# RWKV-7 attention followed by a cosine-gated MLP: the running product of the decays taken on four chunks at once, by a product tree and over DRAM

## The chip, the cores and the metric

The kernel runs on one core of a Trainium2 chip. The metric is device time in microseconds, the median of several executions of the program. TensorE is called PE, VectorE DVE, ScalarE ACT, GpSimd POOL, and SyncE, which here only issues DMAs, SP. PEld is PE's loading of weights, which overlaps its matmuls.

## What is computed

```python
# r, k, v, w, a, b: (4, 8, 768, 40) float32; w between 0.85 and 0.95
for t in range(S):
    y[:, :, t] = einsum('bhd,bhde->bhe', r_t, state)
    Sa = einsum('bhde,bhe->bhd', state, a_t)
    state = state * w_t[:, :, None, :] - einsum('bhd,bhe->bhde', Sa, b_t) + einsum('bhd,bhe->bhde', v_t, k_t)
x = y.transpose(0, 2, 1, 3).reshape(3072, 320)
h = x @ w_in                 # 320 x 2048
out = (h * cos(h)) @ w_out   # 2048 x 320
```

`moe_w_in` and `moe_w_out` come as 64-bit floats and are rounded to 32 bits on the chip.

## The kernel before

The 768 steps are cut into 24 chunks of 32. A chunk's natural layout (`nat`) has 128 partitions, 4 batches times 32 steps, and 8 heads times 64 places (40 used) along the row; the transposed layout has two heads' places on the partitions and 128 columns (batch, step) for each of four head pairs.

Within a chunk the recurrence becomes matrix algebra, for which the running product W of the decays w over the steps of the chunk is needed in both layouts: in the transposed one to scale a (`aT`), the result (`yt`) and the state (`wc`, the last column), and in the natural one as its reciprocal `rw`, which scales b (`bn`) and k (`kn`).

The work before the recurrence goes by pairs of chunks and is called p1. Its steps are:

- `p1_w(c)`: PE transposes w of both chunks into one PSUM tile `wT` (line 298). ACT copies the first column of each chunk aside (line 336), DVE clears it in PSUM (line 337), and a DVE scan multiplies along the steps (line 340) into `wb`. POOL copies the last columns to `wc`.
- `p1_a(c)`, once for each chunk: PE transposes the scanned `wb` back (`wn`, line 353) and a (`aps`, line 298), both into halves of one PSUM tile; DVE takes the reciprocal of `wn` (line 361) and multiplies `aps` by the product shifted by one step (line 363); POOL multiplies b by the reciprocal (line 366).
- `p1_b(c)` and `p1_n(c)`: `bn` is transposed, copied by ACT, and multiplied with `aT` (`nps`); ACT copies the result to `nt`.

For each four chunks DVE inverts the triangular matrices that come of `nt`: a transpose (`u`, line 406), 31 steps of a product and a subtraction each (lines 414 and 418), and a transpose to `rt` (line 422). `p2` prepares v, r, k of a chunk (`vT`, `rT`, `kT`, `gram`), and `main(c)` is the recurrence proper in five steps: `ch_t` transposes the state (`sT`), then `ch_q`, `ch_x` (`x0ps`), `ch_s` (`sps`, which needs `rt`) and `ch_z` (`dps`, which gives the new state `qz` and the output `yt`). The output goes through DRAM (`xd`) to the layout of the MLP (`xT`).

The MLP is cut into pieces: `first_a` and `first_b` (`ph`), turned into `gT` on ACT and DVE (`turns`), and `second` (`po`). While the recurrence goes on, a piece is put at each place marked M in the list of a chunk's segments, which is written out by hand (`segs`). All engines run their instructions in the order in which this list issues them. `later(n, work)` issues work n steps on. Until chunk 3 the pieces wait for the rounding of the weights (`words`, `mant`, `expo`, lines 205 to 232).

Eight PSUM banks are used: `at()` gives out two tiles of two banks in turn, and `ps_h` and `ps_o` two of one bank each, which hold `ph` and `po`, and in the start-up `wn` and `aps` too. A tile is given out again only when all have read it.

SP issues nearly all loads; the first loads of a go out from ACT and POOL. `shifted(n)` puts n one-column matmuls on PE, before chunk 2 (56) and chunk 19 (48). `busy` puts idle matmuls on PE in the start-up.

The order of the start-up, before chunk 0, is

```python
first, other = p1(0), p1(2)
for seg in (*first[:3], *other[:3], *first[3:], *other[3:]):
    step(seg)
```

Of the kernel before, what the change touches and what calls it, by code (L numbers as in the profile page):

```python
# [20 lines left out]
def kernel(  # L21
# [68 lines left out]
    def kept(name, shape, n=1, fill=None, part=lambda t: t, on=nc.gpsimd):  # L90

        tiles = []
        for i in range(n):
            t = const.tile(shape, F32, tag=f"{name}{i}", name=f"{name}{i}")
            if fill is not None:
                on.memset(part(t), fill)
            tiles.append(t)
        return tiles
# [47 lines left out]
    def load(c, names, via=nc.sync):  # L146
        for n in names:
            for i in range(B):
                via.dma_start(
                    nat[n, c][blk[i], :, :D],  # L150
                    src[n][i, :, c * C : (c + 1) * C, :].rearrange("h t d -> t h d"),
                )

    for c in range(2):
        load(c, "w")
        load(c, "a", nc.scalar)
    for n, c in (("b", 0), ("b", 1), ("w", 2), ("w", 3), ("b", 2), ("b", 3)):
        load(c, n)
    load(0, "kvr")


# [2 lines left out]
    for i in range(4):  # L164
# [1 line left out]
            su[blk[i]], su[blk[i]], pattern=[[0, HH], [1, C]], compare_op=ALU.is_gt, fill=0.0,  # L166
            base=0, channel_multiplier=-1,
        )
    load(2, "a", nc.gpsimd)
    load(3, "a", nc.gpsimd)  # L170
    half_pi = kept("half_pi", [P, 1], 1, math.pi / 2)[0]
    warm = kept("warm", [P, 1])[0]
    nc.scalar.activation(warm, half_pi, ACTF.Sin)
    rnd = kept("rnd", [P, 1], 1, ROUND)[0]
    w1 = kept("w1", [P, 4 * B, C], 2, 0.0, on=nc.vector)
    bn_b = kept("bn", [P, H, DP], 7, 0.0, padding, nc.vector)
    kn_b = kept("kn", [P, H, DP], 2, 0.0, padding, nc.vector)

    by_in = kept("by_in", [P, 1], 1, 0.5 / math.pi)[0]
    by_out = kept("by_out", [P, 1], 1, 2.0 * math.pi)[0]  # L180
# [1 line left out]


    BF16 = mybir.dt.bfloat16
    idle = const.tile([P, 512], BF16, tag="idle", name="idle")
    nc.gpsimd.memset(idle, 0.0)
    tick = const.tile([P, 1], BF16, tag="tick", name="tick")

# [103 lines left out]
    def at(name):  # L292
        return ps_a.tile([P, 2, 512], F32, tag="at", name=name)

    def turned(ps, x):

        for i in range(4):
            nc.tensor.transpose(  # L298
                ps[:, i * P : (i + 1) * P], x[:, 2 * i : 2 * i + 2].rearrange("p e d -> p (e d)"), ident
            )  # L300
# [10 lines left out]
    def later(steps, work):  # L311
        waiting.append([steps, work])
# [17 lines left out]
    def p1_w(c):  # L330
        ps = at("wT")
        for i in range(2):
            turned(ps[:, i], nat["w", c + i])

        for i in range(2):
            nc.scalar.copy(w1[i][:, :, 0:1], b4(ps[:, i])[:, :, 0:1])
        nc.vector.memset(ps[:, :, ::C], 0.0)
        for i in range(2):
            wb = ring.tile([P, 4 * P + 1], F32, tag="wb", name="wb")
            nc.vector.tensor_tensor_scan(wb[:, 1:], ps[:, i], flat(w1[i]), 0.0, ALU.mult, ALU.add)  # L340
            wc = ring.tile([P, 4 * B], F32, tag="wc", name="wc")
            nc.gpsimd.tensor_copy(wc, wb[:, C::C])
            G["wb", c + i], G["wc", c + i] = wb, wc

    def p1_a(c):
        if c < 4:
            wn = ps_h.tile([P, 512], F32, tag="h", name="wn")
            aps = ps_o.tile([P, 512], F32, tag="o", name="aps")
        else:
            ps = at("wn")  # L350
            wn, aps = ps[:, 0], ps[:, 1]
        for j in range(4):
            nc.tensor.transpose(
                wn[:, j * P : (j + 1) * P], G["wb", c][:, j * P + 1 : (j + 1) * P + 1], ident
            )

        nc.gpsimd.memset(G["wb", c][:, : 4 * P : C], 1.0)
        G["wx", c] = b4(G["wb", c][:, : 4 * P])
        turned(aps, nat["a", c])
        rw = ring.tile([P, H, D], F32, tag="rw", name="rw")  # L360
        nc.vector.reciprocal(rw, unpad(wn.rearrange("p (h d) -> p h d", h=H)))  # L361
        aT = ring.tile([P, 4, P], F32, tag="aT", name="aT")
        nc.vector.tensor_tensor(
            aT.rearrange("p j (b t) -> p (j b) t", b=B), b4(aps), G["wx", c], ALU.mult
        )
        nc.gpsimd.tensor_tensor(unpad(bn_b[c % 7]), unpad(nat["b", c]), rw, ALU.mult)
        G["rw", c], G["aT", c] = rw, aT

    def p1_b(c):
        ps = at("bT")  # L370
# [204 lines left out]
    def ch_z(c):  # L575
# [3 lines left out]
        for bb in range(B):  # L579
            for e in range(2):  # L580
                mm(
                    ps[bb // 2][full[e], bb % 2, : 4 * N72], idle[blk[bb], :DP],
                    idle[blk[bb], : 4 * N72], True,
                )
        for s, n in ((0, kn_b[c % 2]), (1, bn_b[c % 7])):
            for j in range(4):
# [145 lines left out]
    def p1(c):  # L732


        def first_w():
            p1_w(c)
            if c == 4:
                for i in range(2):
                    later(1, lambda i=i: load(6 + i, "w"))

        def an_a(i):
            p1_a(c + i)
            if c == 4:
                later(1, lambda: load(6 + i, "ab"))
            elif i and c >= 2 and c + 3 < NCH:
                for m in range(6):
                    later(
                        9 + m // 3 if c == 2 else 2 + m, lambda m=m: load(c + 2 + m % 2, "wab"[m // 2])
                    )

        return [first_w, lambda: an_a(0), lambda: an_a(1), lambda: p1_b(c), lambda: p1_n(c)]

    def p2(c):
        def last():
# [14 lines left out]
    with tc.manual_schedule():  # L769
# [24 lines left out]
        def busy(n, after=False):  # L794


            ps = ps_h.tile([P, 512], F32, tag="h", name="busy")
            if after:
                nc.vector.memset(tick, 1.0)
                nc.tensor.matmul(  # L800
                    ps[:1, :], lhsT=tick, rhs=idle, start=True, stop=True, skip_group_check=True
                )
            for _ in range(n):
                mm(ps, idle[:, :P], idle, True)

        def shifted(n):

# [4 lines left out]


        first, other = p1(0), p1(2)
        for seg in (*first[:3], *other[:3], *first[3:], *other[3:]):
            step(seg)
        p2_in(0)
        p2_kn(0)
        inv_steps.extend(inverse(0))
# [2 lines left out]
        for n, seg in ((12, v), (0, k), (0, g), (6, main(0)[2]), (6, None), (4, v1), (0, k1), (0, g1)):  # L822
            for _ in range(n):
                inv_steps.pop(0)()
            if seg:
                step(seg)
            else:
                for m in range(3):
                    w_work[m][0]()
                p2_in(1)  # L830
                p2_kn(1)
        while inv_steps:
            inv_steps.pop(0)()
            if 2 < len(inv_steps) < 9:
                busy(1, True)
# [13 lines left out]
        def allowed(c):  # L849
            return done < len(pieces) and 2 * pieces[done][0] + 2 <= c  # L850

        N_PAD = {2: 56, 19: 48}
        M = object()
        for c in range(NCH):
            t, q, x, s, z = main(c)
# [3 lines left out]
            if c == 0:  # L859
                segs = [s, z]  # L860
            elif c == 1:
                segs = [t, v, q, k, x, g, s, z]
            elif c == 2:
                segs, fill = [t, v, q, k, M, x, M, g, M, s, M, z, M, M], (0, 2)
            elif c == 3:
                pw4, pa4, pa5, pb4, pn4 = p1(4)
                pw, pa, pa1, pb, pn = p1(6)
                segs = [
                    t, pw4, M, q, pa4, M, x, pa5, M, s, pw, M, pb4, pa, M, pn4, pa1, M, z, M, pb, v,
                    pn, k, M, g,  # L870
                ]
                fill = (2, 3)
            elif c == 4:
                pw, pa, pa1, *p8 = p1(8)
                segs = [t, v, M, q, M, k, x, M, g, M, s, M, z, M, pw, M, pa, pa1, M]
                fill = (2, 0)
            elif c == 5:
                pw, pa, pa1 = p1(10)[:3]
                pb, pn = p8
                segs = [t, M, pb, q, M, pn, v, M, x, k, M, s, pw, M, g, M, z, M, pa, pa1, M]  # L880
            elif c % 4 == 0 and q0 < NCH:
                pb, pn = p1(q0)[3:]
                segs = [t, v, M, q, M, k, x, M, g, M, s, pb, M, z, M, pn, M, M]
            elif c % 4 == 1 and q0 < NCH:
                pw, pa, pa1 = p1(q0 + 2)[:3]
                segs = [t, M, pw, q, M, x, k, M, s, v, M, z, M, pa, M, g, M, pa1, M]
            elif c % 4 == 2 and q0 < NCH:
                pb, pn = p1(q0 + 2)[3:]
                segs = [t, M, pb, q, M, pn, v, M, x, M, s, k, M, g, M, z, M, M]
            elif c % 4 == 3 and q0 + 4 < NCH:  # L890
                fill = (2 if c == 7 else 1, 0)
                pw, pa, pa1 = p1(q0 + 4)[:3]
                segs = [t, M, pw, q, M, x, k, M, s, v, M, z, M, pa, M, g, M, pa1, M]
            else:
                segs = [t, v, M, q, M, x, k, M, g, M, s, M, M, z, M, M]
            n = len(segs)
# [4 lines left out]
                empty = max(0, min(places - (goal - done), 2 if c < 8 else places))  # L901
                goal = max(goal, done + places - empty)
            place = 0
            if c in (2, 19):
                shifted(N_PAD[c])
            for i, seg in enumerate(segs):
                while seg is s and ("rt", c) not in G:
# [56 lines left out]
```

## Time and profile before

| | |
|---|---|
| median of 6 runs | 847.03 us (845.13 to 850.77) |
| the profiled execution: its own time | 845.26 us |
| its span, first to last instruction | 843.2 us |
| PE matmul busy | 750.1 us, 89% of the span |
| DVE busy | 511.8 us, 61% |
| ACT busy | 377.1 us, 45% |
| POOL busy | 197.1 us, 23% |
| moved by DMA | 49.10 MB |

The profile is of one execution. Its views used below are: the span in 40 slices; groups of instructions by line (busy time, mean ns of one, and the engine's idle time just before them with what ended it); the timeline of one engine (start, length, number of instructions, and in brackets the idle time before); and the chain of waits, the work that ended last, followed back. An idle engine costs nothing unless the end waits for it.

### The profile page before, as it was taken

How to read it: one execution, taken by the hardware profiler on the slowest of the kernel's cores; microseconds unless marked ns; L12 is line 12 of the kernel's file. 1: busy time of each engine (PE TensorE's matmuls, PEld its weight loads, DVE VectorE, ACT ScalarE, POOL GpSimd, SP SyncE). 2: the span in 40 equal slices, each digit the busy share in tenths (PEclk: the TensorE clock that was granted, in tenths of full speed). 3: DMA queues.
4: the chain of work that ended last, by engine and by line, in shares of the span. 5: the costliest groups of instructions: out<-in, count | busy, mean ns of one | idle time of the engine just before them, and what ended most of it. 6: DMA issues, size and time to landing. Idle time of an engine off the chain costs nothing.

```text
span 843.2 us, 37597 instructions
## 1 busy us (share of the span) xinstructions
PE 750.1 (89%) x16820; PEld 577.2 (68%) x16830; DVE 511.8 (61%) x1076; ACT 377.1 (45%) x707; POOL 197.1 (23%) x343
## 2 busy tenths in 40 slices
PE   3546687995898989999998999998999999999997
PEld 3424466774676767787776777776777877777775
DVE  8688878779534796335796345796355774323331
ACT  1216676353253433546344436435445444454343
POOL 4305634230303203212221221230221222011000
PEclk9758698998999999999999999999999999999999
DMA  7456453431233223324224214214211211101000
GB/s 99 84 100 188 126 156 86 65 66 34 41 52 59 58 36 56 61 36 71 52 38 77 50 24 67 60 37 73 55 25 37 44 35 42 35 20 35 19 16 16
DMA packets 181856, 49.10 MB, mean 58 GB/s; under 512 B 156992, under 2 KB 178496, under 8 KB 181696
## 3 DMA queue, kind: packets, MB, share of 16 engines
q1 hardware_dynamic: 179264, 46.05, 27.3%
q8 instruction: 132, 2.16, 1.1%
q10 hardware_dynamic: 2176, 0.33, 0.3%
q0 software_dynamic: 256, 0.33, 0.2%
q14 instruction: 28, 0.23, 0.1%
HBM read 38.80 MB, written 7.86 MB: 55 GB/s over the span
## 4 chain that ended last, share of the span: by engine, by line
PE 66%; DVE 23%; ACT 5%; issue 3%; DMA 2%; POOL 0%; SPq 0%; ACTq 0%; DVEq 0%
PE ph L101 23%; PE po L101 19%; DVE inv_tmp L414 5%; DVE inv L418 5%; PE x0ps L101 3%; PE dps L101 3%; PE gram L101 2%; PE vT L298 2%; PE sps L101 2%; PE nps L101 2%; DVE rw L361 2%; PE qps L101 1%; PE sT L504 1%; DVE turns L678 1%; DVE wb L340 1%
## 5 line engine op out<-in xcount | busy, mean ns | idle before, releaser
L101 PE MATMUL po<-w_out_sb,gT 128*128 128x320 f32 x768 | 226.6, 442 | 0.0
L101 PE MATMUL ph<-xT,w_in_sb 128*128 128x256 f32 x768 | 191.6, 396 | 4.9 <-DVE gT L686 3.7
L101 PEld LDWEIGHTS po<-w_out_sb,gT 128*128 128x128 f32 x768 | 141.3, 192 | 54.3 <-issue 3.5
L101 PEld LDWEIGHTS ph<-xT,w_in_sb 128*128 128x128 f32 x768 | 143.7, 195 | 33.9 <-issue 13.4
L676 ACT ACTIVATE turns<-ph,rnd 128x512 f32<-128x512 f32 x96 | 63.8, 685 | 160.4 <-PE ph L101 160.0
L678 DVE SCALAR_TENSOR_TENSOR turns<-turns,ph 128x512 f32<-128x512 f32 x96 | 63.8, 684 | 111.7 <-ACT turns L676 111.5
L603 POOL TENSOR_TENSOR qz<-qz,wc 128x160 f32<-128x160 f32 x92 | 42.6, 480 | 253.6 <-DVE qz L602 252.9
L686 DVE TENSOR_TENSOR gT<-ph,turns 128x512 f32<-128x512 f32 x96 | 65.8, 687 | 36.8 <-ACT turns L683 36.8
L414 DVE TENSOR_TENSOR inv_tmp<-u,inv 128x31 f32<-128x31 f32 (+15 forms) x186 | 71.2, 383 | 4.4
L418 DVE TENSOR_TENSOR inv<-inv,inv_tmp 128x31 f32<-128x31 f32 (+15 forms) x186 | 68.8, 370 | 6.4
L683 ACT ACTIVATE turns<-turns,half_pi 128x512 f32<-128x512 f32 x96 | 69.3, 722 | 3.1
L682 ACT ACTIVATE turns<-turns 128x512 f32<-128x512 f32 x96 | 60.2, 627 | 21.8 <-DVE turns L678 21.8
L361 DVE RECIPROCAL rw<-wn 128x320 f32<-128x320 f32 x24 | 51.6, 2152 | 7.9 <-PE wn L298 7.6
L101 PE MATMUL ph<-xT,w_in_tail 64*128 64x256 f32 x384 | 54.5, 402 | 0.0
L602 DVE TENSOR_TENSOR qz<-dps,qz 128x160 f32<-128x160 f32 x92 | 29.2, 318 | 32.5 <-PE dps L101 32.4
L508 ACT COPY s<-sT 128x512 f32<-128x512 f32 x46 | 24.6, 586 | 51.6 <-PE sT L504 51.6
L101 PEld LDWEIGHTS ph<-xT,w_in_tail 64*128 64x128 f32 x384 | 33.2, 186 | 10.5 <-issue 7.1
L614 POOL TENSOR_TENSOR yt<-yt,wb 128x512 f32<-128x512 f32 x24 | 31.2, 1301 | 22.3 <-DVE yt L609 22.3
L436 POOL COPY vp<-nat_v 128x320 f32<-128x320 f32 x25 | 12.1, 484 | 98.5 <-DMA nat_v<-in_v_dram 44.6
L101 PEld LDWEIGHTS sps<-x,rt 32*32 32x32 f32 x1536 | 18.0, 111 | 22.2 <-issue 16.9
L101 PE MATMUL sps<-x,rt 32*32 32x72 f32 x1536 | 22.7, 243 | 11.7 <-DVE rt L422 11.2
L520 ACT COPY qz<-qps 40x512 f32<-40x512 f32 x46 | 26.6, 578 | 13.9 <-PE qps L101 13.5
(117 smaller groups left out, 1050.1 us busy)
## 6 DMA issues: line engine op xcount, KB each, us to landing
words<-in_moe_w_in_dram SPq DMA_DIRECT2D x8, 512.0 KB
nat_k<-in_k_dram SPq DMA_DIRECT2D x96, 40.0 KB
nat_v<-in_v_dram SPq DMA_DIRECT2D x96, 40.0 KB
nat_r<-in_r_dram SPq DMA_DIRECT2D x96, 40.0 KB
xd<-yt SPq DMA_DIRECT2D x48, 80.0 KB
out_dram<-ot SPq DMA_DIRECT2D x24, 160.0 KB
nat_w<-in_w_dram SPq DMA_DIRECT2D x88, 40.0 KB
nat_b<-in_b_dram SPq DMA_DIRECT2D x88, 40.0 KB
```

Source lines behind the costliest of these rows:

```text
L101: nc.tensor.matmul(o, lhsT=lhsT, rhs=rhs, start=start, stop=stop, skip_group_check=True)
L361: nc.vector.reciprocal(rw, unpad(wn.rearrange("p (h d) -> p h d", h=H)))
L414: nc.vector.tensor_tensor(tmp, u[:, j : j + 1, :j].to_broadcast([P, C - j, j]), x[:, j:, j : j + 1].to_broadcast([P, C - j, j]), ALU.mult,)
L418: nc.vector.tensor_tensor(x[:, j:, :j], x[:, j:, :j], tmp, ALU.subtract)
L602: nc.vector.tensor_tensor(z, pick(dp, 0, (2 * N72 + C, 2), (N72, 2), (1, D)), z, ALU.add)
L603: nc.gpsimd.tensor_tensor(z, z, wc.rearrange("p (f m b) -> p f m b", f=2, m=2)[:, :, :, bb] .unsqueeze(3).to_broadcast([P, 2, 2, D]), ALU. ...
L614: nc.gpsimd.tensor_tensor(yt.rearrange("p j b t -> p (j b) t"), yt.rearrange("p j b t -> p (j b) t"), wx, ALU.mult)
L676: nc.scalar.activation(n, u, ACTF.Identity, bias=rnd, scale=1.0)
L678: nc.vector.scalar_tensor_tensor(n, n, -ROUND, u, ALU.add, ALU.subtract)
L682: nc.scalar.activation(n, n, ACTF.Abs)
L683: nc.scalar.activation(n, n, ACTF.Sin, bias=half_pi, scale=-2.0 * math.pi)
L686: nc.vector.tensor_tensor(gT[:, 2 * e : 2 * e + 2].rearrange("p f t -> p (f t)"), us[e], ns[e], ALU.mult)
```

## The change

W is no longer made by a scan for each chunk in the transposed layout. w of four chunks (number q of six) is loaded into a tile `ws` with 128 partitions, one for each batch, head and chunk, and 32 steps of 40 places along the row, 655 KB in all. A tree of nine DVE products in place makes the running product along the steps: five upwards on 16, 8, 4, 2 and 1 places of 40, four downwards on 1, 3, 7 and 15. The result is stored to a DRAM tile `wd`, and the loads of w into the natural layout, four a chunk in runs of 160 bytes as before, now read `wd`.

So `nat_w` holds W. `p1_w` transposes it and ACT copies it to `wb`; the scan, its memset and the side copy are gone. The reciprocal reads `nat_w` directly, and the four `wn` transposes of each chunk are gone. `p1_a` now does both chunks: a's eight transposes first, then both products, with the second chunk's reciprocal behind them (in the start-up each reciprocal stands ahead of its product). `over_w` holds the reciprocal and POOL's product.

The tree of q = 0 stands in the start-up; that of q = 1 after both first p1 pairs; q = 2 in chunk 3, q = 3 at the end of chunk 4, q = 4 and 5 at the ends of chunks 8 and 12. Its store is issued one step later, and the next fetch three steps later.

The first loads are spread over SP, ACT and POOL, a of chunk 1 to 3 on POOL. The start-up's order changes, with a of chunks 2 and 3 behind b and n of the first pair. The 56 one-column matmuls before chunk 2 go, 128 come into the first inverse, and those at chunk 19 become 79. `idle` shrinks to 128 columns and is read four times over. The memsets of `bn` and `kn` go from DVE to POOL.

```diff
     def load(c, names, via=nc.sync):
...
-                    src[n][i, :, c * C : (c + 1) * C, :].rearrange("h t d -> t h d"),
-                )
+                at_c = wd[c // 4][i, :, c % 4] if n == "w" else src[n][i, :, c * C : (c + 1) * C, :]
+                via.dma_start(nat[n, c][blk[i], :, :D], at_c.rearrange("h t d -> t h d"))
+    def ws_fetch(q, via=nc.sync):
+        n = 4 * C * D
+        via.dma_start(
+            ws.rearrange("p t d -> p (t d)"),
+            bass.AP(w.tensor, w.offset + q * n, [[S * D, B * H], [C * D, 4], [1, C * D]]),
+        )
+    def ws_scan(q):
+        n = 1
+        while n < C:
+            to = ws[:, 2 * n - 1 :: 2 * n]
+            nc.vector.tensor_tensor(to, to, ws[:, n - 1 :: 2 * n], ALU.mult)
+            n *= 2
+        n = C // 4
+        while n:
+            to = ws[:, 3 * n - 1 :: 2 * n]
+            nc.vector.tensor_tensor(to, to, ws[:, 2 * n - 1 : C - 1 : 2 * n], ALU.mult)
+            n //= 2
+    def ws_store(q):
+        wd[q] = dram.tile([B, H, 4, C, D], F32, tag="wd", name="wd")
+        nc.sync.dma_start(wd[q].rearrange("b h c t d -> (b h c) (t d)"), ws.rearrange("p t d -> p (t d)"))
+    ws_fetch(0)
+    load(0, "b")
+    load(0, "a", nc.scalar)
+    load(1, "b", nc.scalar)
+    ws_scan(0)
+    ws_store(0)
     for c in range(2):
-        load(c, "w")
-        load(c, "a", nc.scalar)
-    for n, c in (("b", 0), ("b", 1), ("w", 2), ("w", 3), ("b", 2), ("b", 3)):
-        load(c, n)
+        load(2 * c, "w")
+        load(2 * c + 1, "w", nc.scalar)
+    ws_fetch(1)
+    load(3, "b", nc.scalar)
+    load(2, "b")
     load(0, "kvr")
...
-    load(2, "a", nc.gpsimd)
-    load(3, "a", nc.gpsimd)
+    for c in range(1, 4):
+        load(c, "a", nc.gpsimd)
...
     def p1_w(c):
...
-            nc.vector.tensor_tensor_scan(wb[:, 1:], ps[:, i], flat(w1[i]), 0.0, ALU.mult, ALU.add)
+            nc.scalar.copy(wb[:, 1:], ps[:, i])
...
+            nc.gpsimd.memset(wb[:, : 4 * P : C], 1.0)
+            G["wx", c + i], G["wc", c + i] = b4(wb[:, : 4 * P]), wc
+        if c >= 4:
+            over_w(c)
+    def over_w(c):
+        rw = ring.tile([P, H, D], F32, tag="rw", name="rw")
+        nc.vector.reciprocal(rw, unpad(nat["w", c]))
+        nc.gpsimd.tensor_tensor(unpad(bn_b[c % 7]), unpad(nat["b", c]), rw, ALU.mult)
+        G["rw", c] = rw
     def p1_a(c):
...
-        for j in range(4):
-            nc.tensor.transpose(
-                wn[:, j * P : (j + 1) * P], G["wb", c][:, j * P + 1 : (j + 1) * P + 1], ident
-            )
...
+        for i in range(2):
+            turned(ps[i], nat["a", c + i])
+        for i in range(2):
+            if c < 4:
+                over_w(c + i)
+            aT = ring.tile([P, 4, P], F32, tag="aT", name="aT")
+            nc.vector.tensor_tensor(
+                aT.rearrange("p j (b t) -> p (j b) t", b=B), b4(ps[i]), G["wx", c + i], ALU.mult
+            )
+            G["aT", c + i] = aT
+        if c >= 4:
+            over_w(c + 1)
...
+    def scanned(q):
+        ws_scan(q)
+        later(1, lambda: ws_store(q))
+        if q == 1:
+            for i in range(2):
+                later(2, lambda i=i: load(4 + i, "w"))
+        if q + 1 < NCH // 4:
+            later(3, lambda: ws_fetch(q + 1))
...
-        for seg in (*first[:3], *other[:3], *first[3:], *other[3:]):
+        for seg in (*first[:2], other[0], *first[2:], *other[1:]):
             step(seg)
+        scanned(1)
...
+        N_PAD = {0: 128, 19: 79}
+        shifted(N_PAD[0])
         while inv_steps:
...
-        N_PAD = {2: 56, 19: 48}
...
             elif c % 4 == 3 and q0 + 4 < NCH:
...
-                segs = [t, M, pw, q, M, x, k, M, s, v, M, z, M, pa, M, g, M, pa1, M]
+                segs = [t, M, pw, q, M, x, k, M, s, v, M, z, M, pa, M, g, M, M]
```

## Prediction

> **What bounds the kernel now.** I read the page's forty slices first. The rows are the busy tenths of the engines, PEclk the clock granted to TensorE, and DMA and GB/s the load of the sixteen DMA engines. A slice is 21 us.
>
> ```profile
> PE   3546687995898989999998999998999999999997
> ...
> DVE  8688878779534796335796345796355774323331
> ...
> PEclk9758698998999999999999999999999999999999
> DMA  7456453431233223324224214214211211101000
> GB/s 99 84 100 188 126 156 86 65 66 34 41 52 59 58 36 56 61 36 71 52 38 77 50 24 67 60 37 73 55 25 37 44 35 42 35 20 35 19 16 16
> ```
>
> Two regimes: up to slice 10 (210 us) VectorE (DVE) is the fuller one and PE has holes; from there PE is nearly full, and only PE work and PE waits count. Next the groups of instructions by line: what leaves, and the nearest kinds to what comes.
>
> ```profile
> L340 DVE TENSOR_TENSOR_SCAN wb<-wT,w 128x512 f32<-128x512 f32 x24 | 28.1, 1212 | 0.4
> ...
> L353 PE MATMUL wn<-ident,wb 128*128 128x128 f32 x96 | 17.0, 306 | 10.1 <-DVE wb L340 8.5 <-DVE yt L609 1.4
> ...
> L467 ACT COPY kT<-kT 128x512 f32<-128x512 f32 x24 | 13.9, 580 | 4.1 <-PE kT L298 3.7
> ...
> L336 ACT COPY w<-wT 128x16 f32<-128x16 f32 x24 | 3.1, 188 | 26.4 <-PE wT L298 26.4
> ```
>
> The 306 ns of a transpose is its latency; what it costs a full PE is its pitch. The PE timeline shows that, and PE's waits (start, length; in brackets the idle time before and who ended it):
>
> ```profile
> 12.10 1.12 PE L353 MATMUL wn<-ident,wb 128*128 128x128 f32 x4 [1.77 <-DVE wb L340]
> 13.01 1.06 PE L298 MATMUL aps<-ident,nat_a 128*128 128x128 f32 x4
> 13.86 1.06 PE L353 MATMUL wn<-ident,wb 128*128 128x128 f32 x4
> ...
> 144.76 1.08 PE L353 MATMUL wn<-ident,wb 128*128 128x128 f32 x4 [3.90 <-DVE wb L340]
> ...
> 255.98 0.60 PE L353 MATMUL wn<-ident,wb 128*128 128x128 f32 x4
> 256.42 0.60 PE L298 MATMUL wn<-ident,nat_a 128*128 128x128 f32 x4
> ...
> 259.90 1.06 PE L504 MATMUL sT<-ident,qz 128*128 128x128 f32 x8 [2.01 <-DVE aT L363]
> 262.16 3.55 PE L101 MATMUL ph<-xT,w_in_sb 128*128 128x256 f32 x8 [1.19 <-DMA xT<-xd]
> ...
> 452.39 0.63 PE L298 MATMUL vT<-ident,vp 128*128 128x128 f32 x4 [3.78 <-DVE aT L363]
> ...
> 575.36 0.63 PE L298 MATMUL vT<-ident,vp 128*128 128x128 f32 x4 [3.78 <-DVE aT L363]
> ```
>
> Four transposes take 0.44 us late (255.98 to 256.42) and 0.85 early (13.01 to 13.86). After 331 us PE waits only at 452 and 575 (3.78 each) and for about 1 us besides. Last the chain of waits, whose DMA steps are the only sight of what a transfer takes:
>
> ```profile
> 2.23 2.91 DMA nat_w<-in_w_dram
> ...
> 257.56 2.38 DMA xd<-yt
> 260.00 2.11 DMA xT<-xd
> ```
>
> **The sum, stage by stage**, is made against the profiled execution: span 843.2, own time 845.26, so 2.06 us lie outside the span. The median of the six runs, 847.03, is 1.77 higher.
>
> *The first product's way through DRAM* is the loss. Now the first reciprocal starts at 13.25 us on DVE, and the inverse's transpose u at 31.66: 18.4 later. New: fetch (655 KB), tree, store (655 KB), then loads of 160-byte runs, in series. No row shows such a transfer. The fastest slice moves 188 GB/s with the DMA engines 0.6 busy, 313 GB/s if busy throughout, so the bytes take 2.1 to 3.5 us, on top of a fixed 2.4 (the 80 KB store above). The fetch lands at 0.8 + 2.4 + 2.1 = 5.3 (6.7). DVE's start-up memsets end at 5.25 (those of w1, bn and kn leave DVE), so they hide in it. The tree: the inverse's products cost 0.19 us at 31 elements and 0.42 at 256, so 0.16 + 1.02 ns an element; nine products of 2,280 elements in all make 3.75, with 0.035 between them 4.07. Tree done at 9.4 (10.8), store at 13.9 (16.7); four loads, issued 0.49 apart, with 2.91 from the last issue to its landing, put w of chunk 0 at T = 18.3 (21.1).
>
> From T on: reciprocal of chunk 0 to T+2.3; its aT waits for eight w transposes, ACT's 0.58 copy, POOL's 0.3 and a's transposes until T+3.05; aT, reciprocal, aT to T+6.4; reciprocal of chunk 2 to T+8.5. Chunk 2's a transposes now stand on PE behind chunk 0's nps, which needs bn of chunk 1: until T+10.5. aT, reciprocal, aT to T+13.9; bn, bT, copies, nps, nt about 4.4 more: u at T+18.3. As long as now, so the shift is T - 13.25: +5.0 or +7.8; **+6.0** taken (T = 19.3). The low end, both bulk transfers like the 80 KB store, is +2.8.
>
> The Trainium skill ("DMA: Bandwidth & Descriptors", "Anatomy of one DMA") gives 2.0 us plus bytes at 436 GB/s; an estimate by it puts T near 17 and the shift near +3.5.
>
> The second tree (4.07) fills DVE's gap between the last aT and u: free with 0.3 us to spare. SP's queue is in order: the second store waits for that tree, to about 37 us, and behind it stand k, v, r of chunk 1 (now issued from 29.68), w of chunks 4 and 5, a fetch, and the weights' words. From 29.68 to 65.09 SP issued 54 DMAs, 0.66 each; now 55 from 37.3, so the fourth weight tile goes out at 73.6 and lands by 76.5. DVE wants it at 74.61 + 6.0 = 80.6. Cost nothing, with 4 us of slack; beyond that each microsecond is one on the path. ACT issues sixteen more loads before its first copy, until about T, and then a 1.3 us table load, all inside the eight transposes. bn's and kn's memsets fall in POOL's idle time before 12 us.
>
> PE sits idle until T. The first transposes run at 0.85 for four against 0.44 later although PEclk shows 9, so they are slow already, and a later start does not slow them more. The rule in "TensorE: Matmul & The Clock Gate" (Part 1: half clock until about 3.4 us of activity) speaks against the longer idle; were PE warm now, it would add some 3.9 us as an estimate, which the pitch rows exclude.
>
> *Pads.* The 56 before chunk 2 took 1.54 us; about 0.3 of it is covered by POOL's qz: **-1.2**. The 128 new ones (3.5 to 7 us) stand where PE idles 6.27 us for tick: nothing. At chunk 19, 31 more at 27.5 ns on a full PE: **+0.8**.
>
> *Chunk 3 (135 to 178 us).* aps no longer waits for a scan, only for ACT's two copies of wT (ending near 142.9): of 3.90 about 1.9 stay saved; 1.3 of waiting for aT before wT goes; four times 0.44 of transposes, 1.8. That is 5.0. DVE does four scans less (4.9) and a tree more (4.07), but had 11 us of idle here. The weights share these engines, so **-4** (bounds -1 to -6). The next inverse fills DVE from 178 to 211 unchanged, so this gain passes through it. One wait is added on SP: w of chunk 7 now also waits until DVE's reciprocal of chunk 5 has read that buffer, near 150, and behind it stand a and b of chunks 6 and 7 (issued from 146.7 now). They come some 4 us later; a of chunk 6 is transposed at 162.5, so nothing is paid.
>
> *Chunk 4.* The wait of 1.77 for aT before sT and 0.9 of transposes go, but the tree behind the reciprocal of chunk 9 holds turns back some 2 us at 231, and a po waits: **-1.5** (0 to -2.7). *Chunk 5*: two groups of four transposes (0.88) and the 2.01 wait leave, but ph at 262.16 waits for xT, whose chain starts at dps: the time turns into that wait, **0**.
>
> *Chunk 7.* From 287 to 320 DVE has no gap; a reciprocal (2.15) replaces two scans (2.43) there, so only 0.28 of PE's 5.3 us of waiting goes, and behind it 0.87 of transposes and a 0.41 wait: **-1.5** (0 to -3).
>
> *Chunks 14 to 23.* Ten times 0.44 is 4.4. The two 3.78 waits arise because sT or vT takes the PSUM slot of a second wn tile, which is only read once DVE reaches a reciprocal late in a full stretch (411 to 456). Afterwards both aT come first, the second reciprocal follows them, and one tile less is taken: both go, -7.6. DVE's load in that stretch falls by 2.4. The trees of chunks 8 and 12 stand where DVE is a third busy. ACT's 24 copies of 580 for 188 ns (+9.4) fall in its 55% idle. **-12.0**.
>
> Sum: +6.0 - 1.2 + 0.8 - 4 - 1.5 - 1.5 - 12.0 = -13.4. Span 829.8, own time 831.9, and with 1.77 the median **833.6**, called 834.
>
> **Rivals.** *Slower: the bulk transfers crawl.* For: the whole span moves 58 GB/s, and the first slices have their DMA engines 0.7 busy with short runs. At 58 GB/s 655 KB take 11.3 us: fetch at 14.5, tree to 18.6, store at 32.3, T = 36.7, a shift of +23.4: 847.0 - 13.4 + 17.4 = 851.0. It breaks even at T = 32.7 and is slower beyond the bound below from T = 35.2. Against: 188 GB/s is seen where runs are long.
>
> *About equal: the waits only move.* PE is saved its transposes, but the waits return under other names (copies by ACT, turns behind a tree). Then +6.0 - 1.2 + 0.8 - 1 - 0.4 - 0.9 - 4.4 = -1.1: 845.9. For: that is what chunk 5 does. Against: after 331 us ACT and DVE have slack around both places.
>
> *More: the start is cheap.* Shift +2.8, chunk 3 at -6, chunk 4 at -2.7: -19.8, 827. For: the 80 KB store's 2.38 with little payload.
>
> **How the numbers follow.** Forecast 0.66, slower 0.15, equal 0.08, more 0.11. The range is 824 to 848: it takes in the forecast's bounds, the equal and the cheap case, and leaves out the slow one and a little below. A difference under 0.3% (2.5 us) is about what cannot be told from none. Faster 0.77, same 0.08, slower 0.15.
>
> **What would show it.** The first reciprocal at 17 to 21 us and u some 18.3 later; no idle before vT where 3.78 stood; aps near 143 with a short wait for ACT; PE's group wn gone; sps behind the first inverse about 6 us later than 61.7 now. Wrong if the first reciprocal starts after 30 us, if DVE waits for words after 69 us, or if new PE waits of 3 us stand in the last two thirds.

## The result, and the profile after

The change made the kernel no faster, and 0.2% slower: 849.5 us in the median of 35 runs (845.81 to 851.89), against 847.37 for the kernel before in 72 runs beside it. The ratio is 1.002, with a 95% interval of 1.001 to 1.003. The prediction was 834, with a range up to 848. The profiled execution of after took 850.85 (span 849.1), that of before 845.26 (span 843.2); single executions of the kernel before lie up to 9.4 us apart, so the difference of the two profiles, 5.9 in the span, is larger than that of the medians, 2.1.

The PE timeline after (start, length; in brackets the idle time before and who ended it), with the lines that answer to those shown of before:

```profile
20.34 1.94 PE L331 MATMUL wT<-ident,nat_w 128*128 128x128 f32 x8 [20.34 <-DMA w_in_sb<-wd]
...
150.87 1.97 PE L331 MATMUL aps<-ident,nat_a 128*128 128x128 f32 x8 [1.99 <-ACT wb L369]
...
195.80 3.78 PE L101 MATMUL ph<-xT,w_in_sb 128*128 128x256 f32 x8 [5.39 <-DMA xT<-xd]
...
225.25 1.46 PE L101 MATMUL sps<-x,rt 32*32 32x72 f32 x64 [8.37 <-DVE rt L458]
...
248.62 1.31 PE L101 MATMUL nps<-aT,bT 40*32 40x32 f32 x128 [2.17 <-ACT bT L411]
...
252.73 4.23 PE L101 MATMUL po<-w_out_sb,gT 128*128 128x320 f32 x8
...
462.39 0.63 PE L331 MATMUL vT<-ident,vp 128*128 128x128 f32 x4 [0.54 <-DVE vvm L529]
...
579.48 0.63 PE L331 MATMUL vT<-ident,vp 128*128 128x128 f32 x4 [0.52 <-DVE vvm L529]
...
681.83 0.34 PE L101 MATMUL gram<-rT,vT 40*32 40x32 f32 x27 [1.00 <-issue]
...
682.92 4.11 PE L101 MATMUL po<-w_out_sb,gT 128*128 128x320 f32 x8
```

Before, sps of chunk 4 was at

```profile
211.44 1.25 PE L101 MATMUL sps<-x,rt 32*32 32x72 f32 x64 [9.57 <-DVE rt L422]
```

The two waits of 3.78 in the later part are gone (0.54 and 0.52 are left), as predicted. New is a wait of 5.39 for xT at 195.80, and sps of chunk 4 starts at 225.25 where before it started at 211.44.

The start of sps is a mark in every chunk. Its time after less its time before, taken from both PE timelines in us (+ is later), gives each stage its gain or loss; u is the transpose at the head of the inverse of chunks 4 to 7 on DVE:

| from, to | shift at its end | measured | predicted |
|---|---|---|---|
| start to sps of chunk 0 | +7.8 | +7.8 | +6.0 |
| to sps of chunk 2 (pads gone) | +8.0 | +0.2 | -1.2 |
| chunk 3, to u | +6.7 | -1.3 | -4 |
| u to sps of chunk 4 | +13.8 | +7.1 | 0 |
| to sps of chunk 5 | +17.0 | +3.2 | -1.5 |
| to sps of chunk 7 | +16.8 | -0.2 | 0 |
| to sps of chunk 8 | +15.2 | -1.5 | -1.5 |
| chunks 8 to 18 | +2.3 | -12.9 | -12.0 |
| chunk 19 | +5.9 | +3.6 | +0.8 |
| sum (before rounding) | | +5.9 | -13.4 |

The largest surprise lies between u and sps of chunk 4. The timeline of DVE after, with the reciprocal of chunk 5 and a line from the middle of the inverse:

```profile
156.27 2.13 DVE L380 RECIPROCAL rw<-nat_w 128x320 f32<-128x320 f32 x1
...
203.21 0.69 DVE L714 SCALAR_TENSOR_TENSOR turns<-turns,ph 128x512 f32<-128x512 f32 x1 [6.28 <-ACT turns L712]
```

and the same place before, where DVE has no idle time:

```profile
190.35 1.28 DVE L678 SCALAR_TENSOR_TENSOR turns<-turns,ph 128x512 f32<-128x512 f32 x2
```

After the change DVE stands 6.28 us in the middle of the inverse, ahead of a turns that belongs to the MLP, because ph, from which it is made, waited for xT. Why xT was late is seen on the timeline of SP, whose rows are issues of DMAs (start, length of issuing, number). First before:

```profile
140.90 3.98 SPq L149 DMA_DIRECT2D nat_w<-in_w_dram  x8
...
170.75 2.96 SPq L149 DMA_DIRECT2D nat_a<-in_a_dram  x4
175.26 0.69 SPq L623 DMA_DIRECT2D xd<-yt  x2
```

and after:

```profile
151.18 9.25 SPq L151 DMA_DIRECT2D nat_w<-wd  x8
...
178.02 4.78 SPq L151 DMA_DIRECT2D nat_w<-wd  x8
182.90 4.92 SPq L151 DMA_DIRECT2D nat_a<-in_a_dram  x8
...
190.82 0.74 SPq L659 DMA_DIRECT2D xd<-yt  x2
```

The eight loads of w of chunks 6 and 7 began when the reciprocal of chunk 4 ended (151.1) and were through only after that of chunk 5 (158.4), for they overwrite what the two read. SP's waits after, between 140 and 200 us (us in total, times, longest), name that releaser:

```profile
SPq L151 <- DVE rw L380: 8.1, 2, 5.3
```

What SP issues later stands behind them. When POOL ended yt of chunk 3 at 181.65, SP was in the loads of chunks 8 and 9 and issued the store 9.2 us later.

The order on SP had changed too. These loads are issued a fixed number of steps behind the last step of `p1_a` for chunks 6 and 7. That was a step of its own for chunk 7 (`pa1`); now one step does both chunks, and it stands earlier in chunk 3. Before, 12 of the 24 loads of w, a and b of chunks 8 and 9 stood ahead of the store of chunk 3's output; after, 20 do.

### The profile page after: what moved, and what is told of

It reads as the page before. It is cut to its first block, busy times and chain, and to the rows that moved or that the text cites. A ratio compares the mean times of both kernels' runs of the same rounds, so it can differ in the third digit from the quotient of the medians.

```text
span 849.1 us, 37671 instructions
## 1 busy us (share of the span) xinstructions
PE 746.5 (88%) x16837; PEld 572.1 (67%) x16837; DVE 506.2 (60%) x1083; ACT 384.2 (45%) x706; POOL 201.6 (24%) x356
## 3 DMA queue, kind: packets, MB, share of 16 engines
q8 instruction: 132, 2.16, 1.1%
## 4 chain that ended last, share of the span: by engine, by line
PE 61%; DVE 16%; DMA 7%; SPq 6%; ACT 4%; issue 3%; POOL 2%; ACTq 0%; DVEq 0%; POOLq 0%
PE ph L101 22%; PE po L101 19%; SPq L151 5%; DVE inv_tmp L450 3%; PE dps L101 3%; PE x0ps L101 3%; DVE inv L454 3%; DVE rw L380 2%; PE gram L101 2%; PE vT L331 2%; PE sps L101 2%; PE qps L101 2%; DMA xd<-yt 1%; DVE turns L714 1%; PE nps L101 1%
## 5 line engine op out<-in xcount | busy, mean ns | idle before, releaser
L101 PE MATMUL ph<-xT,w_in_sb 128*128 128x256 f32 x768 | 189.7, 393 | 13.0 <-DMA xT<-xd 9.2
L101 PEld LDWEIGHTS po<-w_out_sb,gT 128*128 128x128 f32 x768 | 143.2, 194 | 56.3 <-issue 4.8
L454 DVE TENSOR_TENSOR inv<-inv,inv_tmp 128x31 f32<-128x31 f32 (+15 forms) x186 | 71.4, 384 | 6.4
L450 DVE TENSOR_TENSOR inv_tmp<-u,inv 128x31 f32<-128x31 f32 (+15 forms) x186 | 69.5, 374 | 4.6
L380 DVE RECIPROCAL rw<-nat_w 128x320 f32<-128x320 f32 x22 | 47.2, 2143 | 10.6 <-DMA w_in_sb<-wd 10.6
```

The source lines that it names most:

```text
L101: nc.tensor.matmul(o, lhsT=lhsT, rhs=rhs, start=start, stop=stop, skip_group_check=True)
L380: nc.vector.reciprocal(rw, unpad(nat["w", c]))
L450: nc.vector.tensor_tensor(tmp, u[:, j : j + 1, :j].to_broadcast([P, C - j, j]), x[:, j:, j : j + 1].to_broadcast([P, C - j, j]), ALU.mult,)
L454: nc.vector.tensor_tensor(x[:, j:, :j], x[:, j:, :j], tmp, ALU.subtract)
```

## Experiments

Theory: this queue is the main loss besides the start-up (7.1), and the start-up and the tree in chunk 4 add the rest. Rivals: DVE's own load by the tree in chunk 3 delays the inverse; or the start-up is hidden and other things count. Ratios are to the kernel before run beside each; 0.1% is 0.85 us.

**e1: the second reciprocal earlier.**

```diff
         if c >= 4:
             over_w(c)
+        if c == 4:
+            over_w(5)
...
-        if c >= 4:
+        if c > 4:
             over_w(c + 1)
```

> One thing is moved against the changed kernel: DVE's reciprocal of chunk 5 stands directly behind that of chunk 4 instead of behind both aT. Theory (SP's queue): in the changed kernel w of chunks 6 and 7 is issued from 151.18 to 160.4 because it waits for these two reciprocals (148.96 to 151.1 and 156.27 to 158.4), and all that SP issues later, the store of chunk 3's output (190.82 instead of 181.65, when it was ready) among it, comes late by that; ph waits 5.39 for xT, and DVE, in order, stands 6.28 inside the inverse of chunks 4 to 7. Here the second reciprocal ends near 153.3, 5 us earlier: the output's store goes out near 185.8, the wait of ph falls to 1 us or less, and sps of chunk 4 starts 4 to 5 us earlier than 225.25; the time falls by about 4.5, to 845. Rival (DVE's load, with the tree of q = 2 in chunk 3, is what delays the inverse): DVE does the same work, sps of chunk 4 stays within 1 us of 225.3 or comes 2 later since aT stands behind one more reciprocal; 849.5 to 851.5.

843.96 us, ratio 0.9961 (0.9942 to 0.998). SP's eight loads took 3.98 instead of 9.25, the store went out at 186.84, ph waited 2.40 (1 or less was expected), sps of chunk 4 started at 220.78. No work was taken from DVE, so its load is not the cause.

From u to sps of chunk 4 it takes 36.07 here, against 40.19 after and 33.11 before: the wait for the second reciprocal is some 4 of the 7.1, by one execution of each. yt was ready at 181.33, so the store was still 5.5 late. Two things are left that no run takes apart: the loads of w still begin only when the reciprocal of chunk 4 has ended, and 20 loads instead of 12 stand ahead of the store.

**e2: the store ahead of the loads of chunks 8 and 9.**

```diff
-    8 + m // 3 if c == 2 else 2 + m, lambda m=m: load(c + 2 + m % 2, "wab"[m // 2])
+    8 + m // 3 if c == 2 else 8 + m if c == 6 else 2 + m, lambda m=m: load(c + 2 + m % 2, "wab"[m // 2])
```

> One thing is moved against the changed kernel: the loads of w, a and b of chunks 8 and 9 are issued six steps later, so that on SP chunk 3's output (its store and the loads of xT) stands in front of them; the wait of w of chunks 6 and 7 for the reciprocals stays. Theory (SP's queue): SP is through the fetch of q = 3 at 178, so the store goes out when POOL ends yt (181.65), 9.2 us earlier; xT is there by 190.2, ph starts without a wait over 0.7, the 6.28 of DVE's standing goes, rt is ready 33 us after u as in the kernel before (211.3 - 178.33), so sps of chunk 4 starts near 218.2 instead of 225.25; time 842.5 (849.5 less 7). Rival (DVE's load): the wait at ph goes but the inverse ends no earlier than 223, since other things hold DVE; time 848 to 850. Second rival: the late loads of chunks 8 and 9 become a wait of wT or aps in chunk 4, which gives back more than 3 us.

842.66 us, ratio 0.9938 (0.9916 to 0.9961): 0.82% below after, 7.0 us. The timeline of SP in e2, where yt was ready at 182.39:

```profile
182.42 0.70 SPq L659 DMA_DIRECT2D xd<-yt  x2
```

Its PE timeline has no wait at ph, and sps at the predicted time:

```profile
190.98 1.89 PE L101 MATMUL ph<-xT,w_in_sb 128*128 128x256 f32 x8
...
218.54 1.37 PE L101 MATMUL sps<-x,rt 32*32 32x72 f32 x64 [9.43 <-DVE rt L458]
```

The wait of w for the reciprocals is still there (SP's eight loads take 9.48), but with the store not behind it u to sps of chunk 4 takes 32.77, less than before. No wait for the loads of chunks 8 and 9 appeared in chunk 4.

**e8 and e9: the same into the kernel before.** If a late store alone does this, it must do so without any of the change.

```diff
-        later(2, lambda: tokens(c, yt))
+        later(7 if c == 3 else 2, lambda: tokens(c, yt))
```

> The kernel before with one thing moved: the store and the loads of chunk 3's output are issued five steps later, behind the loads of a of chunk 9 and of b of chunks 8 and 9. It puts into the kernel before, without any of the change, only the late output. Theory (a late output of chunk 3 holds ph, and DVE, in order, stands inside the inverse of chunks 4 to 7): the store goes out near 183 instead of 175.26, ph, which wants xT at 183.75, waits 7 to 8, DVE stands 6 or more ahead of the turns at 190.35, and sps of chunk 4 starts near 218.5 instead of 211.44; the time is 854 (1.008 of before). Rival (the late output alone is covered by other pieces or by the inverse's own length, 33 us, and the loss in the changed kernel has another cause): sps of chunk 4 within 2 of 211.4, time 847 to 849.

849.54 us, ratio 1.002 (1.0 to 1.0039). The expectation was wrong: without the hold SP was through the loads at 181.05, and ph waited only 0.66 for xT. The slack of the kernel before was just used up. From sps of chunk 3 to that of chunk 4 it takes 55.81 against 55.62 before, so what the 0.2% comes from, if it is there, is open. e9 adds the hold, 14 stores that nothing needs:

```diff
+    held = dram.tile([P, 14 * D], F32, tag="held", name="held")
...
+        if c == 3:
+            for i in range(14):
+                nc.sync.dma_start(held[:, i * D : (i + 1) * D], ident[:, :D])
         xd = dram.tile([DM, P], F32, tag="xd", name="xd")
```

> e8 with more of a hold: in the kernel before, the output of chunk 3 is issued five steps later, as in e8 (849.54; ph waited only 0.66 for xT there, so its slack is just used up), and 14 small stores that nothing needs (20 KB each, to a scratch in DRAM) stand on SP directly in front of it, 0.48 us of issue each, 6.7 in all. Theory: ph of chunk 4 waits 6 to 7.5 for xT, DVE stands nearly as long inside the inverse ahead of turns, and sps of chunk 4 starts about 62 after sps of chunk 3 instead of 55.8 in e8; the time is 855.5 (1.0095 of the kernel before). Rival (DVE's inverse has slack, or other pieces cover): ph waits as long, but sps of chunk 4 comes less than 2 later, 851.

856.76 us, ratio 1.0112 (1.0093 to 1.0131). On SP the 14 stores took 9.14 and the output's store went out at 190.42, where after has 190.82. The timeline of PE in e9:

```profile
194.97 3.78 PE L101 MATMUL ph<-xT,w_in_sb 128*128 128x256 f32 x8 [7.71 <-DMA xT<-xd]
...
223.83 1.25 PE L101 MATMUL sps<-x,rt 32*32 32x72 f32 x64 [8.36 <-DVE rt L422]
```

and of DVE:

```profile
201.96 0.69 DVE L683 SCALAR_TENSOR_TENSOR turns<-turns,ph 128x512 f32<-128x512 f32 x1 [8.19 <-ACT turns L681]
```

Chunk 4's sps comes 65.9 after chunk 3's (157.93), against 55.8 in e8. The time is 0.92% above e8. With e2 that shows the mechanism: a store that is late on SP by more than its slack stops DVE inside the inverse. (The 14 stores hold what else is behind them on SP as well; no other wait of PE for a load appears up to sps of chunk 4.)

**e3: no way through DRAM in the start-up.**

```diff
-    at_c = wd[c // 4][i, :, c % 4] if n == "w" else src[n][...]
+    at_c = wd[c // 4][i, :, c % 4] if n == "w" and c >= 4 else src[n][...]
...
-    ws_fetch(0)
...
-    ws_scan(0)
-    ws_store(0)
```

> Left out against the changed kernel: the running product of chunks 0 to 3, with its fetch, tree and store; these chunks load w itself. All instructions on PE, ACT and POOL stay. It prices the way through DRAM in the start-up. Theory: the transpose u starts near 31.7 to 32.5 instead of 39.10 and sps of chunk 0 near 62 instead of 69.47; the shift of 7.4 is carried by PE, DVE and SP alike to sps of chunk 4 (near 218 instead of 225.25) and to the end: 842. Rival (the start-up is hidden: the rounding of the weights or SP's queue sets chunks 2 and 3): sps of chunk 0 comes earlier but sps of chunk 4 by less than 3, and the time stays above 846.5.

849.55 us, ratio 1.0009 (0.9993 to 1.0025): nothing. But u came at 37.86, only 1.24 earlier, so the question was not answered. The timeline of ACT in e3, from the end of its loads on:

```profile
18.57 1.28 ACT L204 ACT_TABLE_LOAD   x1 [18.57 <-DMA w_out_sb<-in_b_dram]
...
19.97 2.03 ACT L366 COPY wb<-wT 128x512 f32<-128x512 f32 x4
```

w was there by 9.85 (the first reciprocal), but ACT issues 20 loads before it copies anything, and the copies of wT came at 19.97. The change lays two things side by side in the start-up that end at about the same time: after, w comes at 20.3 and ACT is through its loads at 20.24. e3 shows that ACT's loads alone hold the start until about 20 us. The way through DRAM alone was not run.

**e11: that, with the first loads as before.** On top of e2; also without the first product.

```diff
...
+    for c in range(2):
+        load(c, "w")
+        load(c, "a", nc.scalar)
+    for n, c in (("b", 0), ("b", 1), ("w", 2), ("w", 3), ("b", 2), ("b", 3)):
+        load(c, n)
+    ws_fetch(1)
...
```

> e2 (842.66) with the running product of chunks 0 to 3 left out (they load w itself), and with the first loads in the order and on the queues of the kernel before: ACT issues only a of chunks 0 and 1. All of PE, DVE (but the first tree), ACT's copies and POOL's products stay as in the changed kernel. In e3, without the product but with the changed kernel's loads, ACT was still issuing loads until 18.57 and made its first copy at 19.97, and u came only at 37.86. Theory (the start is set by when w and ACT are there, either of them): the first copy of wb by ACT comes near 10.5, u at 28 to 32, sps of chunk 0 near 58 to 62 instead of 70.2, the time 832 to 835. Rival (the new order of the start-up, a and b of chunks 2 and 3 behind the first nps and the second tree ahead of u, costs the time): u not before 35, sps of chunk 0 not before 66, time above 839.

833.48 us, ratio 0.9836 (0.9816 to 0.9856), 8.6 us below e2 by the ratios. The timeline of DVE in e11 has u, behind the second tree (25.92 to 31.19), at

```profile
31.11 1.24 DVE L436 STREAM_TRANSPOSE u<-nt 128x1024 f32<-128x1024 f32 x1
```

and sps of chunk 0 starts at 61.75 instead of 70.22 in e2: 8.5 earlier, paid in full at the end. It is where the kernel before has it (61.70), so the new order of the start-up costs nothing that is seen. e11 leaves out work that the result needs: its 8.6 is the price of the two things together, not a gain to be had as it stands.

**e6: the old start-up.** On top of e2: the scan for chunks 0 to 3.

```diff
+    for c in range(2):
+        load(c, "w")
+        load(c, "a", nc.scalar)
...
+        if c < 4:
...
+                nc.vector.tensor_tensor_scan(wb[:, 1:], ps[:, i], flat(w1[i]), 0.0, ALU.mult, ALU.add)
...
-        for seg in (*first[:2], other[0], *first[2:], *other[1:]):
+        for seg in (*first[:2], *other[:2], *first[2:], *other[2:]):
```

> On top of e2 the start-up is undone: chunks 0 to 3 get the running product by the scan in the transposed layout, as in the kernel before, with its loads, transposes and order; the tree is kept from q = 1 on, with the second tree behind the first pairs; 112 one-column matmuls instead of 128 in the first inverse, since 16 transposes come back on PE. Theory (the start is paid in full: all that follows hangs on u): u starts at 31.7 to 32.5 instead of 39.1 and sps of chunk 0 near 62 instead of 70.2; chunk 3 and the next inverse move with it, so sps of chunk 4 starts near 211 instead of 218.54, and the time is 835 (842.66 less 7.5; 0.985 of before). Rival (what e3 showed, where the start gained 1.2 and the time nothing: something between chunk 0 and chunk 4, the words of the weights or the queue of SP, takes the place): sps of chunk 0 comes 7 earlier, sps of chunk 4 by less than 3, and the time stays above 840.

835.94 us, ratio 0.9869 (0.9838 to 0.9899), 5.8 below e2 by the ratios. sps of chunk 0 starts at 63.43, of chunk 4 at 211.90: 6.8 and 6.6 earlier than in e2. The start-up is not hidden.

**e5: the third tree moved.** On top of e2.

```diff
-    segs = [t, v, M, q, M, k, x, M, g, M, s, M, z, M, pw, M, pa, lambda: scanned(3), M]
+    segs = [t, v, M, q, M, k, x, M, g, M, s, M, z, M, pw, M, pa, M]
...
-    segs = [t, M, pb, q, M, pn, v, M, x, k, M, s, pw, M, g, M, z, M, pa, M]
+    segs = [t, M, pb, q, M, pn, v, lambda: scanned(3), M, x, k, M, s, pw, M, g, M, z, M, pa, M]
```

> On top of e2 (the loads of chunks 8 and 9 six steps later; 842.66 us, 0.9938 of the kernel before) one thing is moved: the tree of q = 3 stands in chunk 5 behind the step that prepares v and r, where DVE is idle for 8.6 us in e2 (243.96 to 252.55), instead of at the end of chunk 4, where it runs from 234.56 to 238.9. Theory: there it holds DVE's turns (PSUM's ph was there at 234.82), behind them ACT's cosine and, in ACT's order, the copies of bT; so nps waits 2.17 and vT 1.06, PE drops to a low clock and the next po takes 4.32 instead of 2.42. In the new place these go, sps of chunk 5 starts about 3.3 earlier against sps of chunk 4 (35.76 between them in e2, 32.42 in the kernel before), and the time is 839.4 (0.990 of before). Rival: the tree has to stand somewhere, and holds x or the next turns in its new place by as much: 842.7. Second rival: the wait of ph for xT (3.77 at chunk 6) grows by what is gained.

836.37 us, ratio 0.9882 (0.9838 to 0.9925), 4.7 below e2 by the ratios. From sps of chunk 4 to that of chunk 5 it takes 30.54 instead of 35.76: the waits of nps and vT (2.17 and 1.06) are 0 and 0.43. In the profiled execution, the slowest of the six at 845.32 and 9 above their median, the second rival is there too. The timeline of SP in e5:

```profile
259.08 0.40 SPq L179 DMA_DIRECT2D wd<-ws  x1
264.40 0.61 SPq L160 DMA_DIRECT2D ws<-in_w_dram  x1
265.10 0.88 SPq L659 DMA_DIRECT2D xd<-yt  x2
```

The next fetch waits until the store of the same tile has landed, with chunk 5's output behind it, and ph then waits 7.86 for xT instead of 3.77.

**e7: all three.** 

> e2, e5 and e6 together: chunk 3's output ahead of the loads of chunks 8 and 9, the tree of q = 3 in chunk 5, and the old start-up. Theory: the parts are on one path and add: 842.66 - 3.3 - 7.5 = 831.9 (0.981 of the kernel before). Rivals: if the start is hidden, 839; if the tree is only moved, 835; if neither helps, 842.7.

830.72 us, ratio 0.9805 (0.9775 to 0.9836): about 2% faster than the kernel before, and 1.2 below the sum of the parts that was expected.

**e10: the fetch behind chunk 5's output.** On e7.

```diff
-            later(3, lambda: ws_fetch(q + 1))
+            later(16 if q == 3 else 3, lambda: ws_fetch(q + 1))
```

> e7 (830.72) with one thing moved: the fetch of q = 4 is issued behind the output of chunk 5 on SP. In e7 it stands in front of it, waits until the store of q = 3 has landed (issued 247.81, fetch at 251.44), the output's store goes out at 252.86, and its landing takes 4.0 beside the 655 KB (2.3 in the kernel before); ph waits 5.67 for xT. Theory: the output goes out as soon as yt is ready, about 1.2 earlier, and lands 1.5 sooner; the wait of ph falls to about 3, sps of chunk 6 comes 2.5 to 3 earlier, and the time is 828 (0.977 of the kernel before). Rival (the wait is the chain from dps over yt, xd and xT to ph, as in e2, 3.77, and shrinks by 1 at most): 830.

833.01 us, ratio 0.9808 (0.9788 to 0.9828), the same as e7. The wait of ph fell from 5.67 to 3.76, but an idle 0.93 of PE's issue at 273.95 came in its place, and sps of chunk 5 to 6 takes 36.39 against 36.37. Within the spread of such executions nothing was gained.

**e4 and e12: the pads.** e4 is after with `N_PAD = {0: 128, 19: 48}`.

> One size against the changed kernel: 48 one-column matmuls on PE before chunk 19 instead of 79, as in the kernel before. In the changed kernel 79 of them are followed by an idle 1.00 us of PE in gram (681.83, ended by nothing that the profile shows but PE's own issue) and by a po of 4.11 for eight matmuls instead of 2.42; the shift against the kernel before grows there by 3.6. Theory (the number of instructions ahead decides where PE's issue stalls fall, and a stall costs the clock as well): with 48 the stall falls elsewhere or is covered; if it goes, 0.8 of matmuls, 1.0 of stall and 1.7 of slow po are saved: 846.0. Rival (only the matmuls count): 0.8 less, 848.7, with the same stall of 1 us at another instruction.

849.6 us, ratio 1.0012 (0.9992 to 1.0031): not to be told from after. The stall is there again, 1.04, at sps (682.71), as the rival had it, but the po behind it takes 2.42. e12 is e10 without any pads at chunk 19:

> e10 without the 79 one-column matmuls before chunk 19. They take 2.1 us on a full PE (666.01 to 668.06 in the changed kernel). Theory (they only cost their time; the issue stalls of about 1 us near chunk 19 come in some executions with 79 and with 48 of them): 2.1 less than e10, about 826. Rival (their number keeps stalls of PE's issue away further on): a stall of 1 to 2.5 us and a low clock behind it appear after chunk 19 in the profile, and the time is that of e10 or more.

833.66 us, ratio 0.9832 (0.9811 to 0.9853), no gain. The timeline of PE in e12:

```profile
662.15 0.35 PE L101 MATMUL sps<-x,rt 32*32 32x72 f32 x15 [1.98 <-issue]
662.44 4.11 PE L101 MATMUL po<-w_out_sb,gT 128*128 128x320 f32 x8
```

The 2.1 of pads went and 1.98 of stall with a slow po came, and one of 0.93 at 739.83. The same 79 pads have no stall of over 0.5 near chunk 19 in e1, e2 and e3 and one of 1.00 to 1.41 in after, e5 and e7, so the count alone does not decide; what does stays open.

## Why the prediction was wrong

**The step that failed** is the one on SP in chunk 3. It saw the added wait, w of chunk 7 on the reciprocal of chunk 5 "near 150", and ended: "They come some 4 us later; a of chunk 6 is transposed at 162.5, so nothing is paid." It followed the loads of a and b to their users and stopped there. The same queue carries the store of chunk 3's output, and behind it stand xT, ph, ACT's turns and, since DVE is in order, the inverse. It also did not see that the loads of chunks 8 and 9 move ahead of that store, and it had the delay too small: a of chunk 6 was issued at 160.52 instead of 146.73, 13.8 later, while the path itself was 8.0 later (sps of chunk 2), so 5.8 for 4. (The reciprocal of chunk 5 ran from 156.27 to 158.4; "near 150" holds where the start is not late, as in e11 with 148.09.) Put at nothing, this cost 7.1 (e2 gives back 7.0; e9 makes the same wait anew in the kernel before).

**Chunk 3** gained 3.1 by sps of chunk 3, in the sense predicted (aps waits 1.99 for ACT, as foreseen), but 1.8 went again by u: a of chunk 7, held in the same queue, came late (aps of 169.25 waits 1.94 for it; with the shorter hold of e1 no such wait is left, but one of 1.76 on PE's own issue came at 172.78, so e1 does not show what u would gain).

**Chunk 4** foresaw that the tree holds turns, but not who pays: turns was foreseen to make "a po" wait. It made ACT wait 3.49 for DVE, with bT behind it in ACT's order, then nps (2.17), vT (1.03), and a po at 4.23 instead of 2.42: +3.2 instead of -1.5. e5 shows it: with the tree elsewhere this stage takes 30.54 against 32.42 before, -1.9.

**The start-up** was near in size (+7.8 for +6.0, inside the bounds), but only half of its cause was seen. The first reciprocal came at 20.32 (19.3 predicted). The second tree, "free with 0.3 us to spare" at 4.07, took 5.4 and ended after the last copy of nt (38.35), so u waited 0.75 for it. And beside the way through DRAM stood a second hold of the same length: ACT's loads, taken to end "inside the eight transposes", would have held the start by themselves (e3).

**Pads**: the 31 more at chunk 19 cost 0.8 by sT, as computed; the stall and the slow po behind it, 2.8, were not foreseen. Of the 56 taken out nothing is seen by sps of chunk 2 (+0.2 for -1.2).

**Right** were chunk 5 (0.0 for 0; the wait moved to xT, 3.82), chunk 7 (-1.5 for -1.5; the wait moved to DVE's x, 3.98), and the last part: -12.9 for -12.0, with both waits of 3.78 gone. With e2, e5 and e6 together 16.6 us are gained (e7), but only with the start-up undone and two orders changed; without its +6.0 for the start-up the prediction's sum is -19.4. Of the rivals, the slower one was nearest in time (851.0) by a mechanism that did not occur: the first fetch had landed by 5.79. "The waits only move" was right for chunk 5; in chunk 7 a wait moved too, but the gain of the forecast came.

The estimate by the Trainium skill ("DMA: Bandwidth & Descriptors", "Anatomy of one DMA"), T near 17, was short against 20.32. The page fits its 2.0 us and 436 GB/s to transfers that GpSimd issues, and these went out from SP and ACT. Between the issue of the first store (10.11) and that of the loads that wait for it (15.0) lie 4.9 us, with other loads in the queues.

## What to carry to other kernels

When a wait is added on an in-order queue, follow every entry behind it to its user, and the user's own queue too, until all have arrived; the one that hurt here was a store of another stage. When steps are merged, list what they issued and see which entries change places in the queue. And when a start-up is rearranged, look for the second thing that would hold it if the first were free, before taking either as the price.

## What the runs showed of the hardware

PE's granted clock fell after one stall of 1.00 us and did not after others as long. The granted clock after, by windows (length, PE busy, PEld, DVE, ACT, POOL, PEclk, DMA share, GB/s):

```profile
335.70:339.20 3.50, 3.50 (x24) 2.93 (x24) 3.08 (x7) 0.00 (x0) 3.50 (x6) 1.00 0.05 15
...
682.20:687.00 4.80, 4.80 (x73) 3.33 (x74) 4.07 (x13) 0.76 (x3) 0.00 (x0) 0.64 0.02 3
```

The window from 682.20 lies behind the stall of 1.00, and its eight matmuls of po took 4.11 instead of 2.42. The first window lies behind a stall of 1.35, and the clock stayed at 1.00. Near chunk 19 stalls of 1.04 (e4) and 1.41 (e7) left po at 2.42, and one of 1.98 (e12) was followed by 4.11. The Trainium skill ("TensorE: Matmul & The Clock Gate", Part 1) puts the drop after an idle window of about 3.4 us. No stall here is that long, so the measured length alone is no guide; what else decides, no run here shows.

The profile names no releaser for these stalls. The Trainium skill ("Runtime: NRT & Kernel Launch", "Instruction fetch mechanics") says that instructions come in blocks of 16 KiB and that a crossing is mostly hidden. In the profile after, the larger queue of instructions moved 132 packets and 2.16 MB, 16.4 KB each, which agrees with the blocks; that the stalls are such crossings no run here shows.

The nine products of a tree took 3.95 us at 5.79, where POOL issued loads, and 5.4 at 33.74, beside POOL's copies and products. The other four took 3.9 (three, with POOL nearly idle) and 4.4 (beside one product of POOL). That POOL is the cause fits these numbers, but no run takes POOL's work away alone.
